# When the opening of an attention and token-mixing kernel fetches its first weights: later, and in two parts

## The chip, the cores and the metric

The kernel runs on one core of one Trainium2 chip. The metric is the device time of one execution in microseconds (us). A core has five engines that work side by side: TensorE (PE, matmuls; PEld is its weight load), VectorE (DVE), ScalarE (ACT), GpSimd (POOL) and SyncE (SP), which here only issues DMAs. SP, ACT and POOL issue DMAs, all of which run on the same 16 DMA engines.

## The reference

```
q, k, v: [8 batches, 8 heads, 576 positions, 64]
heads 0..3: each position sees the 32 positions up to itself (local)
heads 4..7: each position sees the earlier positions with the same remainder mod 32 (strided)
x = softmax(q k^T / 8, masked) v                      # [8, 576, 512]
u = x + (relu(x^T w_tok1) w_tok2)^T                   # w_tok1 [576, 256], w_tok2 [256, 576]
out = u + relu(u w_ch1) w_ch2                         # w_ch1 [512, 1536], w_ch2 [1536, 512]
```

The weights come as 64-bit floats.

## The kernel before

The opening computes the attention and the token mixing of batch 0; after it the channel layers run in groups of 512 positions, with the attention and mixing of the later batches and the conversion of the channel weights put between their matmuls. In the opening the order on every engine is the order of the program, written out by hand.

The attention of the opening is cut into eight units. Units 0 to 3 are strided, 4 to 7 local; units 4 and 5 hold three blocks of 128 positions (of batch 0's chunks 0 to 2 of x), units 6 and 7 two. The loop `for k in range(n + 3)` is a pipeline: in pass k, PE does the value matmuls of unit k-3 (`t<-lv,as` for a local unit), the transposes of unit k-2 (L85), four filler matmul records on `ident` (passes 4 to 7) and the score matmuls of unit k (`t<-lk,lq`). VectorE does the outputs of unit k-3 (L194, L195, L257 for a local one, which writes x) and the scores of unit k (L182), ScalarE the copies of unit k-2 (L210) and the exponentials of unit k (L185). From pass 8 on, `mix` multiplies chunk after chunk of x with the first token weight (`t<-x,t1f`). SP stores the strided units' results (`xs<-ax`, L322, L324) and, in pass 6, begins to load them back as the second half of x (`x<-xs`, L432).

The token weights come in six pieces, made by `early(k, f)`. Pieces 0, 1 and 2 are the first token weight, `t1f` (512, 512 and 256 KB); pieces 3, 4 and 5 are the second, `t2f` and `t2e` (512, 512 and 128 KB). A piece is a generator whose steps are taken one at a time by `next`:

- the first `next` issues its DMA from POOL (L155, `w_first<-in_words`);
- the second joins the halves of the 64-bit words: an activation on ScalarE (L136) and a byte copy on POOL (L140) that waits for it;
- the third finishes on VectorE (L147, L150), behind POOL's copy.

Pieces 0, 1 and 2 take their second step in passes 5, 6 and 7 and the third in the pass after. Pieces 3, 4 and 5 take these steps behind the loop. POOL would issue the DMAs as soon as it comes to them; what holds them back is `gate`, a copy of one column that POOL makes before, and that waits for the load it reads. From pass 7 on, `fetch()` issues the pieces of the channel weights (`w_raw<-in_words`, 512 KB each), the first three from POOL, the later ones from SP.

The loads of the inputs are issued in this order, nearly all from SP: eq, ek, ev of the strided units, then lq and lk of the local ones, and last both lv (`local[hp][2]`, L616).

Of the kernel before, what the change touches and what calls it, by code (L numbers as in the profile page):

```python
# [87 lines left out]
class Turns(Banks):  # L88
# [3 lines left out]
    def next(self):  # L92
        self.last ^= 1
        return self.tile(f"h{self.last}")
# [13 lines left out]
def attn_mixer_kernel(ctx, tc, qT, kT, vw, qs, ks, vs, qsT, ksT, vsP, mask, words, outT):  # L108
    nc = tc.nc
# [316 lines left out]
    def load_x(x_t, b, half, c0=0, c1=NSC):  # L426
        cs = slice(HL * D * half, HL * D * half + HL * D)
        if half and b < NPE:

            src = xs[b].rearrange("(r j) d -> r j d", j=NJP)  # L430
            for i in range(4):
                nc.sync.dma_start(out=x_t[ST * i:ST * i + ST, :, cs], in_=src[:, i::4])  # L432
            return
        src = xs[b] if half else xl[b // 2][S * (b % 2):S * (b % 2) + S]
        c = min(c1, NSC - 1)
        nc.sync.dma_start(out=x_t[:, c0:c, cs], in_=src[P * c0:P * c].rearrange("(c p) d -> p c d", p=P))
        if c1 == NSC:
            nc.sync.dma_start(out=x_t[:, NSC - 1, cs], in_=src[P * (NSC - 1):].unsqueeze(0).to_broadcast([2, 64, HL * D]))
# [104 lines left out]
    def fetch():  # L543
        k, what = next(conversion["pieces"], (None, None))
        if what:
            p_ = piece(k, *what)
            next(p_)
            conversion["waits"].append(p_)
# [16 lines left out]
    with tc.tile_pool(name="first", bufs=2) as first, \  # L565
# [10 lines left out]
        def flat(t):  # L576
            return t.rearrange("p c n -> p (c n)").bitcast(U32)

        def early(k, f):
            n = f.shape[1]  # L580
            raw = first.tile([P, n, 2], U32, name=f"w_first{k}", bufs=1)
            fetched(raw, k, nc.gpsimd)
            yield
            yield from joined(raw, f, "pool")
# [18 lines left out]
        local = [[first.tile([P, nq + r], F32, name=n) for n, r in (("lq", 0), ("lk", 32))] + [first.tile([P, nq // 32, D + 1], F32, name="lv")] for _ in range(2)]  # L603
# [11 lines left out]
        for hp in range(2):  # L615
            nc.sync.dma_start(out=local[hp][2], in_=vw[0, hp, :, :nq // 32])  # L616
        gate = first.tile([P, 16], F32, name="gate", bufs=1)
        nc.gpsimd.tensor_copy(out=gate[:, :1], in_=local[0][1][:, :1])
        early_pieces = [early(k, f) for k, f in enumerate((
            flat(t1f[:, 0:2]), flat(t1f[:, 2:4]), t1f[:, NSC - 1].bitcast(U32), t2f[:, 0].bitcast(U32), t2f[:, 1].bitcast(U32), flat(t2e)))]  # L620
        for p_ in early_pieces:
            next(p_)
        units = [strided_unit(None, work, 0, hp, half, strided[hp]) for hp in range(2) for half in range(2)]
        units += [local_unit(None, work, 0, hp, c0, n, x_t, local[hp]) for c0, n in ((0, 3), (3, 2)) for hp in range(2)]
# [3 lines left out]
        def mix(c, half):  # L628
            r = P if c < NSC - 1 else P // 2
            cs = slice(HL * D * half, HL * D * half + HL * D)  # L630
            for m in range(2):
                ps_0.matmul(ph[m][:, cs], t1f[:r, c, P * m:P * m + P], x_t[:r, c, cs], start=(c == 0 and not half), stop=(c == NSC - 1 and not half), skip_group_check=True)

        for k in range(n + 3):
            if k >= 3:
                units[k - 3].send(banks[k - 3])
                next(units[k - 3])
            if 0 <= k - 2 < n:
                b0, b1 = banks[k - 2]
                next(units[k - 2])  # L640
                units[k - 2].send([(b0, 256, 2), (b1, 256, 1)])
            if k == n:
                ph = [ps_0.tile() for _ in range(2)]
            if k < n:
                next(units[k])
                banks.append([ps_0.bank() for _ in range(2)])
            for _ in range(WARM.get(k, 0)):
                ps_0.matmul(banks[k][1].of[:, 512 - P:], ident, ident, start=True, stop=True)
            if k >= n:
                mix(k - n, 0)  # L650
            if k < n:
                units[k].send(banks[k])
                next(units[k])
            if k == 6:
                load_x(x_t, 0, 1)
            for p_ in early_pieces[:3][max(0, k - 6):max(0, k - 4)]:
                next(p_)
            if 7 <= k < n + 2:
                fetch()
        for p_ in early_pieces[3:5]:  # L660
# [225 lines left out]
    for n, t in enumerate(sections):  # L886
        if n <= nu:
            new, out, mid = n if n < nu else None, n - 2 if n > 1 else None, n - 1 if n else None
        elif n == nu + 1:
            new, out, mid = nu, nu - 1, None  # L890
        else:
            new, out, mid = n - 1 if n - 1 < len(units) else None, n - 2, None
# [165 lines left out]
```

## Time and profile before

| | us |
|---|---|
| median of three runs | 809.53 (809.01 to 811.7) |
| profiled execution, its time | 809.25 |
| profiled execution, span from the first to the last instruction | 807.5 |
| PE busy | 787.6 |

The mean granted TensorE clock was 0.996 of full speed. In the views, all times are microseconds from the start of the span, and "idle before <-releaser" is how long an engine stood still before a row and what ended it. "issue" is time in which an engine waited for nothing that the profile shows.

### The profile page before, as it was taken

The page shows a single profiled execution, that of the slowest core. Times are in us where ns is not written, and L with a number is a line of the kernel's source. Part 1 is how long each engine was busy: PE and PEld are TensorE (multiplying, and loading weights), DVE is VectorE, ACT ScalarE, POOL GpSimd, SP SyncE. Part 2 cuts the span into 40 slices and gives each one's busy share as a digit, 9 for nine tenths or more (in the row PEclk, how much of TensorE's full clock was granted, in tenths as well). Part 3 has the DMA queues.
Part 4 walks back from the last instruction along what each step waited for, and adds up shares of the span by engine and source line. Part 5 has one row for each costly group of instructions (what it writes and reads, how often), then busy time and mean ns, then how long its engine had stood idle before and what let it go on. Part 6 is the DMA issues. An engine that isn't in the chain of part 4 may idle for free.

```text
span 807.5 us, 16145 instructions
## 1 busy us (share of the span) xinstructions
PE 787.6 (98%) x6320; PEld 646.4 (80%) x6320; DVE 484.6 (60%) x1752; ACT 239.3 (30%) x561; POOL 252.6 (31%) x258
## 2 busy tenths in 40 slices
PE   6799999999999999999999999999999999999997
PEld 5567778888888878888888888888888888888886
DVE  4687985556467787766766678777776233113122
ACT  6577873233222222222212222222121211111010
POOL 2300000053105782279127932686257000000000
PEclk9899999999999999999999999999999999999999
DMA  9547782345504250335133321334020301001001
GB/s 358 180 140 243 236 273 69 103 144 155 146 1 161 77 148 3 111 102 132 44 104 108 90 87 40 123 91 134 1 83 11 94 3 51 1 0 54 1 0 53
DMA packets 61544, 79.82 MB, mean 99 GB/s; under 512 B 16316, under 2 KB 46908, under 8 KB 61468
## 3 DMA queue, kind: packets, MB, share of 16 engines
q1 hardware_dynamic: 60044, 74.32, 29.9%
q0 software_dynamic: 1136, 4.06, 1.3%
q8 instruction: 50, 0.82, 0.4%
q10 hardware_dynamic: 288, 0.40, 0.2%
q14 instruction: 26, 0.21, 0.1%
HBM read 60.16 MB, written 18.48 MB: 97 GB/s over the span
## 4 chain that ended last, share of the span: by engine, by line
PE 89%; ACT 3%; DVE 3%; DMA 3%; issue 1%; SPq 0%; ACTq 0%; DVEq 0%
PE acc L729 34%; PE h L710 34%; PE t L82 20%; ACT as L185 1%; PE t L85 1%; DMA x<-xs 1%; DMA ek<-in_ksT 1%; ACT w_raw L138 1%; PE h L85 1%; DMA mask_sb<-in_mask 1%; DVE xlo L450 1%; DMA xs<-so 1%; DVE gl L716 1%; DMA w_raw<-in_words 0%; ACT w_a L136 0%
## 5 line engine op out<-in xcount | busy, mean ns | idle before, releaser
L414 POOL TENSOR_TENSOR sprod<-sv,ss 128x512 f32<-128x512 f32 (+9 forms) x150 | 136.3, 947 | 122.4 <-issue 52.5
L710 PE MATMUL h<-uh,w1h 128*128 128x512 f32 x432 | 171.6, 397 | 2.3 <-DVE ul L517 1.4
L729 PE MATMUL acc<-gh,w2h 128*128 128x512 f32 x432 | 170.5, 395 | 0.0
L729 PE MATMUL acc<-gh,w2l 128*128 128x512 f32 x432 | 168.6, 390 | 0.0
L710 PE MATMUL h<-uh,w1l 128*128 128x512 f32 x432 | 168.6, 390 | 0.0
L710 PE MATMUL h<-ul,w1h 128*128 128x512 f32 x432 | 168.4, 390 | 0.0
L729 PE MATMUL acc<-gl,w2h 128*128 128x512 f32 x432 | 168.4, 390 | 0.0
L716 DVE SCALAR_TENSOR_TENSOR gl<-h,gh 128x512 fp32r<-128x512 f32 x108 | 74.4, 689 | 149.0 <-ACT gh L715 148.7
L366 POOL TENSOR_TENSOR sprod<-sk,sq 128x512 f32<-128x512 f32 x80 | 102.2, 1311 | 136.6 <-DVE ss L367 97.3
L715 ACT ACTIVATE gh<-h 128x512 fp32r<-128x512 f32 x108 | 64.9, 601 | 225.5 <-PE h L710 225.5
L710 PEld LDWEIGHTS h<-uh,w1h 128*128 128x128 f32 x432 | 81.1, 188 | 20.9 <-DVE ul L517 2.2
L710 PEld LDWEIGHTS h<-uh,w1l 128*128 128x128 f32 x432 | 81.1, 188 | 17.2
L729 PEld LDWEIGHTS acc<-gh,w2l 128*128 128x128 f32 x432 | 81.1, 188 | 17.2
L729 PEld LDWEIGHTS acc<-gh,w2h 128*128 128x128 f32 x432 | 81.2, 188 | 16.3
L729 PEld LDWEIGHTS acc<-gl,w2h 128*128 128x128 f32 x432 | 81.2, 188 | 15.9
L710 PEld LDWEIGHTS h<-ul,w1h 128*128 128x128 f32 x432 | 81.2, 188 | 15.8
L416 DVE TENSOR_REDUCE so<-sprod 128x64 f32<-128x512 f32 (+9 forms) x150 | 73.7, 526 | 17.5 <-POOL sprod L414 17.5
L185 ACT ACTIVATE as<-as,am 128x64 f32<-128x64 f32 x216 | 55.8, 337 | 67.3 <-DVE am L182 67.3
L367 DVE TENSOR_REDUCE ss<-sprod 128x8 f32<-128x512 f32 x80 | 51.2, 669 | 6.3 <-POOL sprod L366 6.0
L182 DVE CUSTOM_DVE_ANT_0 as<-t,mask_sb 128x64 f32<-128x64 f32 x216 | 34.1, 220 | 33.7 <-PE t L82 27.5
L517 DVE TENSOR_TENSOR ul<-t,uh 128x512 fp32r<-128x512 f32 (+5 forms) x44 | 23.0, 526 | 46.0 <-ACT uh L516 45.9
L82 PE MATMUL t<-t,hh 128*128 128x384 f32 (+5 forms) x184 | 47.9, 342 | 0.0
(106 smaller groups left out, 843.7 us busy)
## 6 DMA issues: line engine op xcount, KB each, us to landing
w_raw<-in_words SPq DMA_DIRECT2D x21, 512.0 KB
lv<-in_vw SPq DMA_DIRECT2D x18, 390.0 KB
out_t<-xh SPq DMA_DIRECT2D x18, 256.0 KB
out_t<-xlo SPq DMA_DIRECT2D x18, 256.0 KB
lk<-in_kT SPq DMA_DIRECT2D x18, 208.0 KB
x<-xl SPq DMA_DIRECT2D x14, 256.0 KB
lq<-in_qT SPq DMA_DIRECT2D x18, 192.0 KB
xl<-ax SPq DMA_DIRECT2D x18, 192.0 KB
```

The costliest lines, as they stand in the source:

```text
L82: self.tc.stamp_issue_order_token(self.tc.nc.tensor.matmul(*args, **how).ins, self.pool.name)
L182: nc.vector.tensor_tensor_reduce(out=s_t[:, c, j, :], in0=sc[j].of[:, 64 * c:64 * c + 64], in1=mask_sb[:, m, :], scale=-SCALE, scalar=TOP, ...
L185: nc.scalar.activation(out=s_t[:, c, j, :], in_=s_t[:, c, j, :], func=AF.Exp, bias=m_t[:, c, j:j + 1], scale=-1.0)
L366: nc.gpsimd.tensor_tensor(out=pr, in0=k_t[:, n0:n0 + n], in1=q_t[:, i:i + 1].to_broadcast([P, n, D]), op=ALU.mult)
L367: return [lambda: nc.vector.tensor_reduce(out=s_t[:, i, n0:n0 + n], in_=pr, axis=AX.X, op=ALU.add)]
L414: nc.gpsimd.tensor_tensor(out=pr, in0=v_t[:, d0:d1, :n], in1=s_t[:, n - 1:n, :n].to_broadcast([P, d1 - d0, n]), op=ALU.mult)
L416: todo.append(lambda n=n, d0=d0, d1=d1, pr=pr: nc.vector.tensor_reduce(out=o_t[:, n - 1, d0:d1], in_=pr, axis=AX.X, op=ALU.add))
L517: nc.vector.tensor_tensor(out=ul, in0=whole, in1=uh.bitcast(F32), op=ALU.subtract)
L710: nc.tensor.matmul(ph, l[:, cc, fs], r, start=(cc == 0 and k == 0), stop=(cc == NCC - 1 and k == 2))
L715: nc.scalar.activation(out=gh, in_=ph, func=AF.Relu)
L716: nc.vector.scalar_tensor_tensor(out=gl, in0=ph, scalar=0.0, in1=gh.bitcast(F32), op0=ALU.max, op1=ALU.subtract)
L729: nc.tensor.matmul(acc[cc], l[:, fc, cs], r, start=(fc == 0 and k == 0), stop=(fc == NFC - 1 and k == 2))
```

## The change

The gate reads the last column block loaded, lv of the second head pair, instead of lk of the first. Behind it only pieces 0, 1 and 2 are issued. Pieces 3, 4 and 5 are issued in pass 6, so that on POOL they stand behind the byte copy of piece 1 and ahead of that of piece 2.

```
-        nc.gpsimd.tensor_copy(out=gate[:, :1], in_=local[0][1][:, :1])
+        nc.gpsimd.tensor_copy(out=gate[:, :1], in_=local[1][2][:, 0, :1])
...
-        for p_ in early_pieces:
+        for p_ in early_pieces[:3]:
             next(p_)
...
             for p_ in early_pieces[:3][max(0, k - 6):max(0, k - 4)]:
                 next(p_)
+            if k == 6:
+                for p_ in early_pieces[3:]:
+                    next(p_)
             if 7 <= k < n + 2:
                 fetch()
```

## Rows read from the trace of the kernel before

**Rows 1.** The page: busy time by engine, and the instruction queue's packets.

```profile
PE 787.6 (98%) x6320; PEld 646.4 (80%) x6320; DVE 484.6 (60%) x1752; ACT 239.3 (30%) x561; POOL 252.6 (31%) x258
...
q8 instruction: 50, 0.82, 0.4%
```

**Rows 2.** Chain that ended last, in order of time: start, length, what.

```profile
19.93 2.73 issue
...
31.40 18.61 PE t L82 x100
...
58.30 3.61 DMA w_raw<-in_words
```

**Rows 3.** Timeline of PE: start, length, engine, line, operation, idle before.

```profile
19.48 0.45 PE L82 MATMUL t<-lk,lq 64*32 64x64 f32 x30
22.67 0.30 PE L82 MATMUL t<-lk,lq 64*32 64x64 f32 x2 [2.73 <-issue]
...
28.93 1.23 PE L82 MATMUL t<-x,t1f 128*128 128x256 f32 x4 [1.70 <-DVE x L257]
```

**Rows 4.** DMA queues, 16.03 to 20.2: packets, MB, share of 16 engines.

```profile
q0 software_dynamic: 423, 1.49, 89.2%
q1 hardware_dynamic: 390, 0.19, 15.4%
```

**Rows 5.** DMA queues, 20.2 to 20.3.

```profile
q8 instruction: 1, 0.02, 59.2%
```

**Rows 6.** Stretches: busy time of each engine, granted clock (PEclk), DMA share, GB/s.

```profile
core 0: us, PE busy (x) PEld busy (x) DVE busy (x) ACT busy (x) POOL busy (x), PEclk, DMA share, GB/s
...
22.95:26.37 3.42, 3.42 (x125) 2.97 (x112) 2.84 (x18) 1.88 (x7) 1.34 (x1) 0.50 0.12 34
...
29.78:33.19 3.41, 3.41 (x56) 2.09 (x61) 1.02 (x7) 1.70 (x5) 0.80 (x2) 0.50 0.86 326
```

**Rows 7.** Timeline of VectorE.

```profile
23.00 0.23 DVE L182 CUSTOM_DVE_ANT_0 as<-t,mask_sb 128x64 f32<-128x64 f32 x1 [2.72 <-PE t L82]
...
23.44 0.42 DVE L147 TENSOR_SCALAR w_first<-w_first 128x512 int32<-128x512 int32 x1
...
26.04 0.22 DVE L182 CUSTOM_DVE_ANT_0 as<-t,mask_sb 128x64 f32<-128x64 f32 x1 [0.43 <-PE t L82]
...
28.17 0.62 DVE L257 TENSOR_TENSOR x<-t,az 128x192 f32<-128x192 f32 x2
...
37.49 0.42 DVE L147 TENSOR_SCALAR w_raw<-w_raw 128x512 int32<-128x512 int32 x1
```

**Rows 8.** Timeline of POOL, its DMA issues included.

```profile
10.73 0.19 POOL L618 COPY gate<-lk 128x1 f32<-128x1 f32 x1 [9.42 <-DMA lk<-in_kT]
10.86 3.37 POOL L155 DMA_DIRECT2D w_first<-in_words  x6
20.46 1.32 POOL L140 COPY w_first<-w_first 128x512 uint8<-128x512 uint8 x1 [6.24 <-ACT t1f L136]
...
27.75 0.75 POOL L140 COPY w_first<-w_first 128x256 uint8<-128x256 uint8 x1 [1.69 <-ACT t1f L136]
28.31 1.57 POOL L155 DMA_DIRECT2D w_raw<-in_words  x3
```

**Rows 9.** Timeline of SP's queue.

```profile
6.97 1.32 SPq L616 DMA_DIRECT2D lv<-in_vw  x2
```

**Rows 10.** DMA queues, 14.7 to 15.2.

```profile
q0 software_dynamic: 37, 0.15, 75.4%
q1 hardware_dynamic: 19, 0.04, 23.6%
```

**Rows 11.** DMA issues, 10.8 to 11.5: count, KB, us from issue to landing.

```profile
w_first<-in_words POOLq DMA_DIRECT2D x1, 512.0 KB, 7.5
```

**Rows 12.** DMA issues, 28.3 to 28.4.

```profile
w_raw<-in_words POOLq DMA_DIRECT2D x1, 512.0 KB, 4.6
```

**Rows 13.** Timeline of ScalarE.

```profile
19.76 0.64 ACT L136 ACTIVATE t1f<-w_first 128x512 f32<-128x512 f32 x1
...
31.76 1.22 ACT L136 ACTIVATE t2f<-w_first 128x512 f32<-128x512 f32 x2
```

## The prediction

> **What bounds the kernel now.** I read the page's busy shares first: PE is busy 98% of the span [rows 1], so a change to an opening stage is worth only what it takes off the time until PE's long unbroken stretch. The chain of waits in order of time then shows where that stretch begins: from 31.40 it is one PE piece of 18.61 us [rows 2], and behind it the channel layers run. Whatever moves the start of the mixing matmuls moves all of it; anything else in the opening is hidden. The chain also has a hole at 19.93, 2.73 us in which PE waits for nothing that the trace names [rows 2].
>
> PE's own timeline shows where that hole lies: 30 of the 32 score matmuls of unit 6 are out, two are missing, and these two start at 22.67 [rows 3]. Their data were there, since the other 30 have the same. What the queues did says what was missing. The page has 50 instruction packets of together 0.82 MB, 16 KB each [rows 1]; 6320 matmuls and as many weight loads over 50 packets are about 253 instructions a packet, so these packets are PE's program. From 16.03 to 20.2 not one came through while the 16 engines were full with the early weight pieces (1.49 MB) and stores [rows 4]; one came at 20.2 [rows 5], and PE went on 2.4 us later. I read the hole as a late piece of program, held up by the 2.4 MB of weight pieces.
>
> After the hole the granted clock is 0.50 (1.2 GHz) from 22.95 to 26.37, and again from 29.78 to 33.19, after PE's other idle time of 1.70 us [rows 3, 6].
>
> What sets the start of mixing, 28.93, is VectorE: PE waits there for x of unit 5 [rows 3]. Back from it on VectorE stand, without a gap but for 0.43 us: piece 1's step, the scores of unit 7, the outputs of unit 4, and first piece 0's step at 23.44 [rows 7]. That is 5.49 us from 23.44 to 28.93, or 5.06 without the 0.43.
>
> **The change part by part.** *The gate.* The one-column copy stays on POOL (0.19 us) and waits for the last input load instead of the first lk [rows 8]. Nothing is queued behind it on POOL but the pieces. SP issues both lv loads by 8.29 [rows 9]; in 14.7 to 15.2 its queue moved 0.04 MB and the pieces already 0.15 [rows 10], so the inputs are all but through. The early limit for the gate is 15.3, the late one 16.5; I take 16.0, since the lk gate, too, opened some tenths after its data. Piece 0 is issued 0.13 us behind it, as now (10.73 and 10.86) [rows 8], so at 16.1 instead of 10.86.
>
> *Piece 0's landing.* Now it takes 7.5 us in full queues [rows 11]. The bounds are 3.6 us, for the same 512 KB from SP in a quiet stretch [rows 2], and that 7.5. Nearest is the same size from POOL's queue beside the x loads, 4.6 us [rows 12], and this I take: landing at 20.7, between 19.7 and 23.6. The Trainium skill, page DMA: Bandwidth & Descriptors, section Anatomy of one DMA, gives about 2.0 us plus the bytes at 436 GB/s, by which an estimate is 3.2 us and a landing at 19.3, and the sum below would be a gain of 2.0 us. Both POOL rows here took longer.
>
> *The hole.* PE's next packet of program is asked for in time that now has only the stores of two units in the queues, the inputs being through and pieces 0 to 2 only just issued (1.28 MB instead of 2.43). I expect the hole to shrink to between 0 and 1.5 us. It costs nothing as long as PE goes on by 21.9, because of the next step.
>
> *What is late next.* ScalarE starts piece 0's step at 19.76 [rows 13]; POOL's byte copy follows at 20.46 and ends at 21.78 [rows 8], 2.02 us after ScalarE's start. Now VectorE comes to that piece only at 23.44, since the unit 6 scores in front of it (23.00 to 23.44) wait for PE's hole [rows 7]. With the hole gone those scores are done at about 20.8, and the copy decides. With piece 0 there at 19.76, VectorE would start at 21.8 and mixing at 21.8 + 5.06 = 26.9, 2.0 us earlier. With it at 20.7, VectorE starts at 22.7 and mixing at 27.8: a gain of 28.93 - 27.8 = 1.1 us. I drop the 0.43, a PE wait at half clock, as that stretch would run at full clock. If it stays, the gain is 0.7.
>
> *Pieces 1 and 2* follow by some 1.3 us each per 512 KB at 400 GB/s: piece 1 at about 22.0. ScalarE reaches it behind piece 0's step, two copies and four exponentials, at about 22.9. Hidden, with 0.9 us to spare.
>
> *The second weight's three issues* (1.15 MB) move behind piece 1's byte copy on POOL. That copy would run from about 23.6 to 24.9, the three issues (0.56 us each, 3.37 over 6 [rows 8]) to about 26.6. Behind them on POOL stand piece 2's copy and the three w_raw issues at 28.31 [rows 8], which lose nothing, as they stood at 27.75 and later before. Piece 3 lands at 29.5 by 4.6 us, pieces 4 and 5 by 31.2. ScalarE starts on them at 31.76 now, so at 30.7 then [rows 13]: hidden, though with only some tenths for piece 4. The first w_raw comes behind them in the same queue, at about 32.5 instead of 32.9, and VectorE needs it at 37.49 [rows 7], after two steps of ScalarE. Hidden by 1.5 us or more. The stores of the strided units, no longer sharing the engines with six pieces, finish sooner, and so can x's second half; PE reads it only after mixing has begun, so this brings nothing.
>
> *Sum.* -1.1 us at mixing; the PE piece from 31.40 on carries it to the end. The profiled execution took 809.25 us, its span is 807.5; so 808.1. The three runs have a median of 809.53, 0.28 above the profiled one, by which the time is 808.4; I say 808.3.
>
> **The rivals.** *The clock goes along.* The second half-clock stretch, 3.41 us of full PE work [rows 6], would cost nothing if PE's idle time fell otherwise, up to 1.7 us more. Against it: with the hole gone PE waits longer for x, from about 24.5 to 27.8, and idle time went ahead of both half-clock stretches. With piece 0 at 19.7 and half of this, the gain is 2.0 + 0.85 = 2.9: 806.6.
>
> *The hole stays.* If the packet of program is late for a reason other than the queue's load, unit 6's scores still end at 23.44 and all is as before, since piece 0 is there by then: 809.5. The queues in that stretch speak against it [rows 4]. The Trainium skill, page DMA: Bandwidth & Descriptors, section Queues, rings and completion order, says that each DMA engine goes round its queues packet by packet; by that a program packet waits for about one 4 KB packet of each, whatever is queued, and this rival would be the likeliest. The trace does not agree: no program packet came in 4.2 us of full engines, and the pieces' own first packets, issued from 10.86, are seen only from 14.7 on [rows 4, 8, 10].
>
> *Piece 0 too late.* It decides once ScalarE's step on it starts after 21.85, that is 5.75 us behind its issue, for then 21.85 + 2.02 + 5.06 = 28.93. At the 7.5 us of now it lands at 23.6 and mixing starts at 30.7, 1.8 us later: 811.3. The stores of units 2 and 3 run beside it, as now; but three pieces, not six, and no inputs are ahead.
>
> **How the numbers follow.** About 0.3%, 2.4 us here, is what a measurement of this kernel can tell from no change. Forecast (gain 0.3 to 2.2 us): 0.55. Clock goes along: 0.17. Hole stays, or comes back at the next packet: 0.13. Piece 0 or the second weight too late: 0.15. The range leaves out the outer half of the first rival and of the last: 806.3 to 810.4. Faster by over 0.3% needs nearly all of the first rival, 0.16; slower by as much needs piece 0 some 8.2 us behind its issue, or a second delay with it, 0.07; the rest, 0.77, lies within 0.3%.
>
> **What would show it.** The gate's copy on POOL at 15.3 to 16.5 and three DMA issues behind it; no PE gap near 20 of over 1.5 us, and a program packet before 19; ScalarE's first t1f step waiting for a DMA until 19.8 to 21.5; VectorE's first L147 behind POOL's copy, not behind PE; first mixing matmul between 26.9 and 28.6; three further POOL issues at about 25, and no wait of ScalarE's t2f steps over some tenths. I am wrong if the hole is still there, if piece 0 takes over 5.75 us, or if a new PE gap opens after mixing begins, say for t2f or the first w_raw.

## The result, and the profile after

The changed kernel takes 817.17 us (median of six runs, 815.82 to 819.29), the kernel before 809.7 in the same job (six runs, 808.56 to 812.35). The ratio is 1.0093, 95% interval 1.0075 to 1.0111: about 0.9% slower. The forecast was 808.3, and its range ended at 810.4. The profiled execution took 818.38 us, the second longest of the six; its span is 816.6, 9.1 more than before, where the medians differ by 7.5.

The timeline of PE in the changed kernel (start, length, engine, line, operation, idle before and what ended it) answers to [rows 3] and shows where the 9.1 us are:

```profile
19.43 0.72 PE L82 MATMUL t<-lk,lq 64*32 64x64 f32 x32
22.88 1.13 PE L82 MATMUL t<-lv,as 64*32 64x65 f32 x48 [2.72 <-ACT as L210]
...
29.35 2.02 PE L82 MATMUL t<-x,t1f 128*128 128x256 f32 x4 [2.19 <-DVE x L257]
...
33.95 1.13 PE L82 MATMUL t<-x,t1f 128*128 128x256 f32 x4
40.38 9.87 PE L82 MATMUL t<-x,t1f 128*128 128x256 f32 x28 [5.30 <-DMA xl<-ax]
50.18 1.09 PE L82 MATMUL t<-ident,x 128*128 128x128 f32 x8
...
60.42 0.50 PE L713 MATMUL h<-uh,w1h 128*128 128x512 f32 x1 [1.40 <-DVE ul L517]
```

The hole of two missing score matmuls is gone: all 32 are out at 20.15. Mixing still starts 0.42 us later than before (29.35 for 28.93), and then a gap of 5.30 us opens that before did not have, ahead of the mixing with x's second half. The same place in the kernel before, from its timeline:

```profile
33.46 7.76 PE L82 MATMUL t<-x,t1f 128*128 128x256 f32 x32
...
41.15 1.10 PE L82 MATMUL t<-ident,x 128*128 128x128 f32 x8
...
51.39 0.50 PE L710 MATMUL h<-uh,w1h 128*128 128x512 f32 x1 [1.40 <-DVE ul L517]
```

The account: mixing starts 0.42 later; from there to the mixing with chunk 2 (the four records at 33.95, before the first four of the row at 33.46) it is 4.60 us for 4.53 (+0.07); from those to the transposes it is 50.18 - 33.95 = 16.23 for 41.15 - 33.46 = 7.69 (+8.54); from the transposes to the first h matmul it is 10.24 both times. Together 9.03 of the 9.1. The 8.54 are the gap of 5.30 and 3.24 that these 32 matmul records themselves take longer. The 28 behind the gap begin with the mixing of x's second half; the program puts the first half's chunks 3 and 4 behind it. The windows say why these take longer (busy time of each engine with instructions, granted clock, DMA share, GB/s):

```profile
core 0: us, PE busy (x) PEld busy (x) DVE busy (x) ACT busy (x) POOL busy (x), PEclk, DMA share, GB/s
...
40.38:50.20 9.82, 9.82 (x29) 7.08 (x29) 2.10 (x4) 2.65 (x4) 0.00 (x0) 0.69 0.36 109
39.63:46.45 6.82, 6.07 (x14) 4.88 (x15) 2.85 (x5) 2.97 (x4) 0.00 (x0) 0.50 0.53 159
```

Behind the gap, in which PE stood still for 5.30 us, the granted clock is 0.50, that is 1.2 GHz, until 46.45, and only then 2.4 GHz again. It is a third half-clock stretch, beside two that answer to [rows 6] (22.56 to 25.97 and 29.38 to 32.80, both at 0.50).

The trace puts the 5.30 us down to `xl<-ax`, the store that landed last by the profile. But the first matmuls behind the gap read x's second half, `x<-xs`, and not `xl`, and in the experiments below the same gap is put down to `x<-xs` by name. SP's queue issues that load:

```profile
17.73 3.02 SPq L322 DMA_DIRECT2D xs<-ax  x4
20.79 0.34 SPq L324 DMA_DIRECT2D xs<-ax  x1
25.98 4.44 SPq L432 DMA_DIRECT2D x<-xs  x4
```

Before, the four issues came at 25.02 and took 2.60. What SP waits for ahead of them are the strided units' stores, for 2.5 us before and 4.6 us in the changed kernel (us in total, times, longest):

```profile
SPq L432 <- DMA xs<-ax: 2.5, 1, 2.5
```

```profile
SPq L432 <- DMA xs<-ax: 4.6, 4, 2.4
```

POOL in the changed kernel, answering to [rows 8]:

```profile
17.26 0.19 POOL L618 COPY gate<-lv 128x1 f32<-128x1 f32 x1 [15.95 <-DMA lv<-in_vw]
17.39 1.79 POOL L155 DMA_DIRECT2D w_first<-in_words  x3
22.62 1.34 POOL L140 COPY w_first<-w_first 128x512 uint8<-128x512 uint8 x1 [3.44 <-ACT t1f L136]
...
26.16 1.58 POOL L155 DMA_DIRECT2D w_first<-in_words  x3
28.04 0.76 POOL L140 COPY w_first<-w_first 128x256 uint8<-128x256 uint8 x1 [0.30 <-ACT t1f L136]
28.60 1.58 POOL L155 DMA_DIRECT2D w_raw<-in_words  x3
```

So x's second half is asked for at 25.98, the second token weight 0.18 us later, and three channel pieces at 28.60. The next view shows what the queues (q1 is SP's, q0 POOL's) moved from 26 to 30 in the kernel before, which had only the w_raw issues behind the load: packets, MB, share of 16 engines.

```profile
q1 hardware_dynamic: 704, 0.66, 60.4%
q0 software_dynamic: 13, 0.05, 16.2%
```

The same four microseconds of the changed kernel, with the size of the load:

```profile
q0 software_dynamic: 143, 0.52, 50.8%
q1 hardware_dynamic: 144, 0.14, 10.7%
...
x<-xs SPq DMA_DIRECT2D x4, 160.0 KB
```

And its next four, 30 to 34:

```profile
q0 software_dynamic: 303, 1.11, 85.5%
q1 hardware_dynamic: 221, 0.20, 18.3%
```

Before, SP's queue moved the whole load of 4 times 160 KB in this stretch. After, by 34 it has moved 0.34 MB, while POOL's queue moved 1.63. A packet of q0 is 3.7 KB here (1.11 MB over 303), one of q1 0.9 (0.20 over 221): the two queues get packets at a like rate (143 to 144, then 303 to 221), and the load with the small packets gets a fifth to a seventh of the bytes. The Trainium skill, page DMA: Bandwidth & Descriptors, section Queues, rings and completion order, says that each DMA engine goes round its queues a packet at a time. The like rate of packets agrees with that, if a packet of the profile is what that section counts as one (several descriptors), which no run here shows. From 39.2 to 40.4, when POOL's burst is nearly through, only 32 packets move; why the last ones come so late is open.

### The profile page after: what moved, and what is told of

Its sections match the earlier page's. It is cut to its first block, busy times and chain, and to the rows that moved or that the text cites. A ratio compares the mean times of both kernels' runs of the same rounds, so it can differ in the third digit from the quotient of the medians.

```text
span 816.6 us, 16145 instructions
## 1 busy us (share of the span) xinstructions
PE 791.1 (97%) x6320; PEld 648.6 (79%) x6320; DVE 486.3 (60%) x1752; ACT 239.3 (29%) x561; POOL 253.5 (31%) x258
## 4 chain that ended last, share of the span: by engine, by line
PE 87%; DMA 5%; DVE 3%; ACT 2%; POOL 1%; issue 1%; SPq 1%; DVEq 0%; POOLq 0%; ACTq 0%
PE acc L732 33%; PE h L713 33%; PE t L82 19%; DMA w_raw<-in_words 1%; DMA ek<-in_ksT 1%; DMA lv<-in_vw 1%; POOL sprod L366 1%; PE t L85 1%; DVE xlo L450 1%; PE h L85 1%; DMA w_first<-in_words 1%; ACT w_raw L138 1%; ACT as L185 0%; DMA xl<-ax 0%; DVE gl L719 0%
```

## The experiments

My first theory after the result was that the second weight's move is the loss: its three fetches meet x's load. The rival was that the gate's move is the loss, by making something late. All kernels are edits of the kernel before or of the changed one, and use these two parts of the change:

```
gate   -  in_=local[0][1][:, :1]            (before: the first lk)
       +  in_=local[1][2][:, 0, :1]         (after: the last lv)
second -  for p_ in early_pieces:  next(p_)
       +  for p_ in early_pieces[:3]:  next(p_)
       +  ...  if k == 6:  for p_ in early_pieces[3:]:  next(p_)
```

The table holds what the traces show, in us: the start of the early fetches, of pieces 3 to 5 where they are apart, of x's second-half load (SP), of the three w_raw (POOL, unless it says SP), PE's gap ahead of the second half's mixing, and the first h matmul, all from one execution of each kernel; then the median (runs) and the ratio to the kernel before in the same job, with its 95% interval.

| kernel | early | 3-5 | x load | w_raw | gap | h | median (n) | ratio |
|---|---|---|---|---|---|---|---|---|
| before | 10.86 | with | 25.02 | 28.31 | 0 | 51.39 | 809.7 (6) | 1 |
| after | 17.39 | 26.16 | 25.98 | 28.60 | 5.30 | 60.42 | 817.17 (6) | 1.0093 [1.0075, 1.0111] |
| gate only | 17.01 | with | 29.46 | 28.86 | 6.63 | 59.44 | 818.0 (4) | 1.0101 [1.0077, 1.0126] |
| second only | 10.93 | 24.99 | 23.07 | 27.12 | 0 | 51.01 | 809.34 (10) | 0.9994 [0.9984, 1.0004] |
| after, w_raw from SP | 17.73 | 26.61 | 26.49 | 29.25 SP | 0.99 | 54.11 | 811.36 (10) | 1.0017 [1.0004, 1.003] |
| gate only, w_raw from SP | 17.04 | with | 29.59 | 32.71 SP | 0.69 | 53.88 | 812.01 (6) | 1.0032 [1.002, 1.0044] |
| after, 3-5 behind x | 17.04 | 32.26 | 26.07 | 33.82 | 0 | 59.53 | 816.24 (4) | 1.0062 [1.0038, 1.0085] |
| before, spare fetches | 10.92 | spare 26.17 | 26.70 | 29.08 | 4.37 | 58.03 | 812.03 (10) | 1.0017 [1.0002, 1.0033] |
| after, filler | 17.10 | 26.24 | 26.40 | 28.44 | filled | 56.61 | 814.6 (4) | 1.005 [1.0035, 1.0065] |
| after, 3-5 a pass earlier | 17.06 | 24.31 | 26.05 | 29.00 | 1.18 | 52.02 | 810.59 (10) | 1.0014 [1.0002, 1.0026] |
| after, gate on the first lv | 16.05 | 26.57 | 25.23 | 29.10 | 0 | 53.55 | 810.64 (10) | 1.0015 [1.0002, 1.0027] |
| gate on lk, 3-5 a pass earlier | 10.86 | 21.90 | 22.73 | 26.83 | 0.67 | 49.34 | 807.9 (6) | 0.9969 [0.995, 0.9988] |
| gate on ev, 3-5 a pass earlier | 9.24 | 21.71 | 22.72 | 26.97 | 0 | 50.32 | 809.13 (12) | 0.9992 [0.9976, 1.0009] |

### Each part alone

The gate only (the `gate` lines on the kernel before, all six pieces behind it).

> The later gate alone, all six pieces behind it. Theory (the loss comes from the second weight moving beside the load of x's second half): the pieces are out by about 26, PE's gap ahead of the second-half mixing stays under 1 us, time 809 to 811.5. Rival (the late first weight is the loss): most of it is here, 815 to 817. Both expect PE's hole near 20 to be another one: no late program packet, but ScalarE waiting for piece 0.

It costs as much as the whole change, 818.0, ratio 1.0101. My first theory fell here. The chain of waits of this kernel names the mechanism, the parts in order of time:

```profile
21.20 8.18 DMA xs<-ax
...
29.46 0.69 SPq L432
...
31.50 8.65 DMA x<-xs
```

The last store of the strided units takes 8.18 us to land beside 2.4 MB of weight pieces. SP cannot issue the load that reads those stores until then, 4.4 us later than before, and by then w_raw is 0.6 us ahead of it. PE:

```profile
40.29 8.98 PE L82 MATMUL t<-x,t1f 128*128 128x256 f32 x28 [6.63 <-DMA x<-xs]
```

The second weight only (the `second` lines on the kernel before, the gate on lk).

> The first weight as before (gate on the first lk), the second weight's three issues in pass 6. Theory: they and the channel weights behind them still share the engines with the load of x's second half; PE's gap ahead of the second-half mixing is 3 to 6 us and the clock is 1.2 GHz behind it, time 814 to 818. Rival (late first weight): 807 to 810, since the first weight is early and fewer bytes are queued ahead of PE's program.

The time is that of the kernel before, 809.34, ratio 0.9994, and not the 814 to 818 that I expected. The weights that run beside the stores are fewer, SP issues x's load at 23.07, 1.92 us ahead of the second weight, and there is no gap:

```profile
27.65 2.04 PE L82 MATMUL t<-x,t1f 128*128 128x256 f32 x4 [1.56 <-DVE x L257]
...
32.22 7.76 PE L82 MATMUL t<-x,t1f 128*128 128x256 f32 x32
...
41.60 3.70 PE L82 MATMUL t<-t2f,hl 128*128 128x512 f32 x8 [0.59 <-ACT hl L677]
```

Mixing starts 1.28 us earlier than before. By the first h matmul 0.38 of it is left: 0.59 went to a wait for ScalarE, which has itself waited 0.66 us for t2f's piece and 0.90 for w_raw.

### Is it contention with x's load?

The changed kernel with the first three w_raw issued from SP, where they stand behind x's load:

```
-        fetched(raw, k, nc.gpsimd if k < EARLY + 3 else nc.sync)
+        fetched(raw, k, nc.gpsimd if k < EARLY else nc.sync)
```

> The changed kernel, with the first three channel-weight pieces (1.5 MB) issued from SP, so behind the load of x's second half in the same queue. Theory: only 1.15 MB instead of 2.7 MB run beside that load, it lands by about 33 to 35, PE's gap falls from 5.3 to under 1.5 us, time 810 to 813. Rival (x's second half is late because the stores it reads are late, or because its issues are held up): the gap stays near 5, 816 to 818.

The gap shrinks from 5.30 to 0.99 us, though x's load is issued half a microsecond later than in the changed kernel and 0.12 us ahead of the second weight. PE comes to this place 1.0 us later here (36.09 for 35.08), so the wait ends 3.30 us sooner, at 37.08 for 40.38. The median is 811.36.

```profile
37.08 6.87 PE L82 MATMUL t<-x,t1f 128*128 128x256 f32 x28 [0.99 <-DMA x<-xs]
```

The same edit on the gate-only kernel:

> The later gate alone (six pieces behind it, as in the run that lost all), with the first three channel-weight pieces issued from SP behind the load of x's second half. Theory now (the gate makes the stores, and so that load's issue, late; the loss is then the meeting of that load with POOL's next burst): with the burst behind it in SP's queue the load takes about 4 us from its issue near 29.5, PE's gap falls from 6.6 to 1 to 2 us, 810.5 to 813. Rival (the late issue alone costs it): the gap stays over 4 us, 815 or more.

The median is 812.01. Here x's load is issued at 29.59, as late as in the gate-only kernel, and still PE's gap is 0.69 instead of 6.63, and it ends at 35.53 instead of 40.29. PE comes to it 1.18 us later here (34.84 for 33.66). So 4.76 of those 6.63 us are w_raw beside the load, and at most 1.87 the lateness by itself. What is left of the loss includes a wait of ScalarE for w_raw of 4.85 us and one of PE for hl of 0.75.

The changed kernel with the second weight held until x's second half is there: in pass 7, behind four small copies that read it.

```
+            if k == 7:
+                for i in range(4):
+                    nc.gpsimd.tensor_copy(out=gate[32 * i:32 * i + 32, 1:6], in_=x_t[32 * i:32 * i + 32, :, HL * D])
+                for p_ in early_pieces[3:]:
+                    next(p_)
```

> The changed kernel, with the second weight (and so the channel weights behind it on POOL) held by a second gate until x's second half has landed. Theory: that load takes about 4 us as before the change, the gap ahead of the second-half mixing goes; the second weight lands at about 35 to 36 and may cost 1 to 3 us at the second token product: 810 to 813. Rival (x late for reasons of its own): the gap stays and the late second weight comes on top, 817 to 820.

The gap is gone, though x's load is issued as late as in the changed kernel (26.07 for 25.98): alone, it is through by 32.13, when the last of the four copies starts. The time is not gone: 816.24, where I expected 810 to 813. The second weight and w_raw are late now (ScalarE waits 3.65 us in all for the one and 1.86 for the other), and the half clock follows the wait that PE has for it instead, 0.50 from 47.05 to 50.40. ScalarE:

```profile
36.26 0.67 ACT L136 ACTIVATE t2f<-w_first 128x512 f32<-128x512 f32 x1 [2.75 <-DMA w_first<-in_words]
```

PE, where the same eight matmuls took 3.60 us before:

```profile
47.05 6.78 PE L82 MATMUL t<-t2f,hl 128*128 128x512 f32 x8 [2.18 <-ACT hl L679]
```

The kernel before with four spare fetches of 256 KB from POOL in pass 6, into tiles that nothing reads:

```
+            if k == 6:
+                for i in range(4):
+                    spare = stage.tile([P, DM], U32, name="w_a", bufs=4)
+                    nc.gpsimd.dma_start(out=spare, in_=words[EARLY + 3 + i, :, :DM // 2].bitcast(U32))
```

> The kernel before, with all six pieces early as they were, and 1.05 MB of channel-weight words fetched once more in pass 6 from POOL into tiles that nothing reads. Theory (sharing the engines is the loss, not when the second weight arrives): PE's gap ahead of the second-half mixing opens, 3 to 5 us, with 1.2 GHz behind it: 814 to 818. Rival (the second weight's own lateness is the loss): 809 to 811, as the weight that is read is early.

In the profiled execution (816.33, the slowest of ten) the fetches came 0.53 us ahead of x's load, and the gap is there, in a kernel with the gate on lk and all weights early. The last store was late in it before any spare fetch (issued at 23.18, in the kernel before at 21.63), and so was x's load, so the run shows the meeting of the two and not what the fetches do by themselves:

```profile
39.30 8.55 PE L82 MATMUL t<-x,t1f 128*128 128x256 f32 x28 [4.37 <-DMA x<-xs]
```

The ten runs spread from 809.76 to 816.33, median 812.03; only the profiled one reached the 814 to 818 that I expected. Two issues half a microsecond apart may come in either order; that this makes the spread was not shown. The kernel before itself took 816.02 and 816.99 in two of its 26 runs in the last job, and 807.80 to 811.03 in the others; no trace of those two was kept.

### The price of the clock

The changed kernel with 16 matmuls of ident by ident, into a bank that is free, ahead of the mixing with the second half.

```
+        for _ in range(16):
+            ps_0.matmul(banks[n - 1][1].of[:, 512 - P:], ident, ident, start=True, stop=True)
```

> The changed kernel, with 16 more filler matmuls on the identity, whose result nothing reads, ahead of the second-half mixing, so that PE works through most of its 5.3 us gap. Theory: the gap's own 5.3 us stay, but the clock behind it is 2.4 GHz, and the 28 mixing records take about 6.8 instead of 9.9 us: 813.5 to 815. Rival (those records are slow for another reason than the clock after idle time): 817 to 818.

```profile
35.97 3.84 PE L82 MATMUL t<-ident 128*128 128x128 f32 x32 [0.27 <-DVE ax L257]
39.65 6.79 PE L82 MATMUL t<-x,t1f 128*128 128x256 f32 x28
```

PE is busy through what was the gap (the timeline has two records for each of the 16), and the 28 matmuls take 6.79 us instead of 9.87, with a granted clock of 1.00. x's load is issued no sooner than in the changed kernel (26.40 for 25.98). The first h matmul comes 3.81 us sooner: 3.08 from these matmuls, 0.73 from their start. The ratio is 1.0050 for 1.0093. So about 3 us of the loss are clock, and most of the rest is the wait itself.

### When the issues stand apart

The changed kernel with pieces 3 to 5 one pass earlier (`k == 5`):

> The changed kernel, with the second weight's issues one pass earlier, behind piece 0's byte copy: about 22.8 instead of 26.2. Theory: they are out by about 28, so that the load of x's second half shares the engines with half as much; gap 1 to 3.5 us, 811 to 815. Rival (the amount beside that load does not matter, its late start does): as the changed kernel, 816 to 818.

The median is 810.59. x's load is as late as in the changed kernel (26.05), but the second weight is 1.74 us ahead of it and w_raw 2.95 behind: the gap is 1.18.

The changed kernel with the gate on the first lv instead of the last (`local[0][2][:, 0, :1]`):

> The changed kernel with the gate on the first lv instead of the second, about 3 us earlier (near 14 instead of 17.3). Theory now: the first weight is out by about 20.5, the strided stores drain before 24.5, the load of x's second half is issued before 25 and so ahead of the second weight's issues; gap under 1.5 us, 808.5 to 811.5. Rival (any gate behind lk, or the second weight in pass 6, costs it): 814 to 818.

The median is 810.64. The gate opened at 15.92, 1.34 us earlier than in the changed kernel. Mixing starts at 29.77, later than there, yet x's load is issued at 25.23, 1.34 us ahead of the second weight, and no gap opens:

```profile
35.30 8.07 PE L82 MATMUL t<-x,t1f 128*128 128x256 f32 x32
```

In the whole table, gaps of over 4 us stand only where POOL puts at least 1.5 MB within 0.7 us ahead of x's load to 2.7 us behind it. With at least 1.3 us between the load and the first fetch behind it, or with w_raw from 2.9 us behind, or on SP, the gap is 0 to 1.2.

### The best order found

The gate on lk, as before, and pieces 3 to 5 in pass 5, behind the byte copy of piece 0:

> The first weight as before (gate on the first lk), the second weight behind piece 0's byte copy, at about 20.5. Theory: PE's program packet is no longer late, the second weight is out by about 26, and the load of x's second half is nearly alone: mixing starts 1 to 2 us earlier, 807 to 809.5. Rival (any fetch behind the first weight meets that load): a gap of over 2 us, 812 or more.

The median is 807.9, ratio 0.9969 [0.995, 0.9988]: faster than both kernels. Three of its six runs took 805.6 to 806.8, three 809.0 to 809.9, so the gain is not in every execution. The mean granted clock of the whole execution was 1.000 in the two fastest, 0.997 in the third and 0.996 in the other three; 0.004 of 806 us is 3.2 us, an estimate of what the half clock costs these, and most of the difference. The profiled one took 805.98. Its POOL and then its PE:

```profile
21.90 1.63 POOL L155 DMA_DIRECT2D w_first<-in_words  x3
...
26.83 1.57 POOL L155 DMA_DIRECT2D w_raw<-in_words  x3
```

```profile
21.68 0.30 PE L82 MATMUL t<-lk,lq 64*32 64x64 f32 x2 [1.54 <-issue]
...
27.45 1.10 PE L82 MATMUL t<-x,t1f 128*128 128x256 f32 x4 [1.21 <-DVE x L257]
...
32.30 6.87 PE L82 MATMUL t<-x,t1f 128*128 128x256 f32 x28 [0.67 <-DMA x<-xs]
```

The last store lands 1.34 us behind its issue here (8.18 in the gate-only kernel). The hole is 1.54 instead of 2.73, mixing starts 1.48 us earlier, and the windows from 22 to 40 show a granted clock of 1.00. Opened still earlier, on ev:

> The first weight earlier still (gate on the strided ev, near 9), the second weight behind piece 0's byte copy, as in the run that came out fastest. Theory now: the stores drain no later than there and PE's program packet meets fewer bytes, so 806.5 to 808.5, and no gap of over 1 us ahead of the second-half mixing. Rival (a first weight that runs beside the local inputs delays the units): mixing starts over 1 us later than in that run, 809 or more.

The median is 809.13, ratio 0.9992: no difference from before. The opening looks the same (x's load at 22.72, mixing at 27.66, no gap), but the first h matmul comes at 50.32 for 49.34. The mean granted clock is 0.63 from 27.60 to 32.20, so part of this stretch ran at the lower level; with the gate on lk it was 1.00 from 27.40 to 32.30. PE's two waits ahead of it were 1.08 and 1.06 us, with the gate on lk 0.81 and 1.21. Why the clock fell in the one and not in the other is open, and so is why none of its twelve runs is below 807.66.

## Why the prediction was wrong, point by point

**The step that failed** is the sentence on the second weight's move that the strided units' stores "finish sooner, and so can x's second half", and that "this brings nothing". Both halves were wrong. Issued 0.84 us earlier (20.79 for 21.63), the last store is through later, as SP's wait shows: behind the gate on lv the engines stand nearly idle and then get the first weight just as the stores come. From 16 to 18.5 the kernel before moved 1.01 MB, 405 GB/s:

```profile
q0 software_dynamic: 255, 0.88, 87.9%
q1 hardware_dynamic: 238, 0.12, 16.5%
```

The changed kernel moved 0.10 MB:

```profile
q1 hardware_dynamic: 166, 0.09, 12.6%
q8 instruction: 1, 0.02, 3.0%
```

What wasn't moved there was moved later. SP issued x's load 0.96 us later, into POOL's next burst, and it landed after mixing's first half was done. I had asked when x's second half is read (after mixing has begun), and not how long it takes with 1.15 MB of second weight issued 0.18 us behind it and three w_raw behind that. The term that I had put at nothing measures 8.54 us: the gap of 5.30 and 3.24 in the matmuls from there on. I had weighed those fetches only against their own readers, where they were hidden as I said.

**The gate** opened at 17.26, outside my 15.3 to 16.5: the last lv landed 9.22 us behind its issue by the chain of waits. For piece 0 this mis-sized term cost nothing: with the gate at 15.92, where I had put it, ScalarE's first step came no earlier, at 22.32. For x's load it did: with that gate the load was issued 1.34 us ahead of the second weight, no gap opened, and the median was 810.64, ratio 1.0015. So the loss needed both, a gate later than I had it and a load that I had put at nothing. Even so mixing started 0.84 us later than before, not 1.1 earlier.

**Piece 0's landing** took 4.49 us, by the chain, for my 4.6: at about 21.9. That this term was right was luck in part: with the issue at 16.05 it took 6.25, and in the other runs with the gate on the last lv ScalarE's step began 4.6 to 5.4 us behind the issue.

**The hole** went as I said as far as the packet goes, and not in its effect. A program packet came in the quiet stretch (the q8 row above), and all 32 score matmuls were out. But PE stood still as long as before, 2.72 us for 2.73. On ScalarE the step that waits for piece 0 stands, in the order of the program, ahead of the copies (L210) that PE's value matmuls need:

```profile
21.91 0.66 ACT L136 ACTIVATE t1f<-w_first 128x512 f32<-128x512 f32 x1 [2.20 <-DMA w_first<-in_words]
22.47 0.52 ACT L210 COPY as<-t 128x256 f32<-128x256 f32 x2
```

I named what piece 0's lateness does to VectorE, and not what is queued behind the waiting step on ScalarE.

**The start of mixing.** VectorE's first step on piece 0 came behind POOL's copy, as I said, 2.09 us behind ScalarE's start (my 2.02):

```profile
24.00 0.43 DVE L147 TENSOR_SCALAR w_first<-w_first 128x512 int32<-128x512 int32 x1 [3.29 <-POOL w_first L140]
```

With my 5.06 us it gives 29.06; measured were 29.35, as the way from there took 5.35. So the rival "piece 0 too late", which decides from 21.85 on, came true at 21.91, by the late gate and not by a slow fetch; it accounts for 0.13 of the 0.42 us, the longer way for the rest. A gain like the 1.1 us that I forecast exists where the early burst is made smaller without the late gate: the second part alone starts mixing 1.28 us earlier.

**The second weight and w_raw** were hidden nearly as said. Pieces 3 to 5 were issued at 26.16 (I said about 25), t2f's steps waited 0.73 us for a load, the first w_raw step 1.55, both on ScalarE, the first while PE mixed x's first half, the second while PE stood in its gap for x.

**The rivals.** The clock did not go along but against: a third half-clock stretch, worth about 3 us by the filler run. The hole's rival, that the packet is late whatever the queue's load, has the runs against it: the hole that ends with the last two score matmuls was 2.73 and 2.64 us with six pieces behind the gate on lk, 1.27 to 1.82 with three pieces behind a gate on ev, lk or the first lv, and 0 to 0.45 in the seven kernels with the gate on the last lv. But my sentence that no program packet came from 16.03 to 20.2 holds for PE's queue q8 alone. The view of [rows 4] has one more row, a packet of another instruction queue, that came in the full stretch:

```profile
q14 instruction: 1, 0.01, 0.5%
```

So full engines do not keep out every such packet, and how they delay q8's was not shown. The rule that I named with this rival, one packet of each queue in turn, goes with the like packet rates under which x's load fell behind.

**The chances.** Slower by over 0.3% had 0.07. The text listed "a new PE gap opens after mixing begins" as what would make it wrong, for t2f or w_raw; it opened, for x.

## What to carry to other kernels

When a burst of fetches is moved, list every load and store in flight beside its new place, not only the fetches' own readers; here a load in packets of 0.9 KB was moved within 5 us of its first issue when nearly alone, and PE got past its wait for it 14.4 us behind that issue when it ran beside a burst in packets of 3.7. A store that a load waits for carries the delay on, so follow store, dependent load, reader as one chain. Here a gate that left the DMA engines idle was paid for later, and one step of ScalarE that waited held up the copies behind it.

## What the runs showed of the hardware that I had not expected

- A load of 4 times 160 KB, done within the four microseconds from 26 to 30 when alone, had moved 0.34 MB in the eight from 26 to 34 beside POOL's fetches. Its share of the bytes went with the packet size, 0.9 KB against 3.7.
- The last store landed 1.34 us behind its issue when only SP's own 0.12 MB moved beside it and 8.18 beside six weight pieces.
- Where the gate waited for lv, ScalarE's first step on piece 0 began at 21.9 to 22.5 with the issue anywhere from 16.05 to 17.73. What sets that landing, and why the last lv was so late, stays open.
